# Router places in DRAM: rows of 64 bytes, zeroed and scattered whole, in place of single 4-byte words

## The chip, the cores and the metric

One core of one Trainium2 chip runs the whole program in one launch. The metric is device time in microseconds (us); lower is better. TensorE does the matmuls (PE in the rows), VectorE is DVE, ScalarE is ACT, GpSimd is POOL, and SP is the engine that issues most of the DMAs. Each engine works through its own instructions in order.

## The reference, cut to what matters

Three layers follow one another. A delta-rule attention over 4 x 8 heads, 768 tokens of width 48, is a recurrence over time:

```python
for t in range(S):
    y[:, :, t] = einsum('bhd,bhde->bhe', q[:, :, t], state)
    v_old = einsum('bhde,bhd->bhe', state, kt)
    state += bt * einsum('bhd,bhe->bhde', kt, vt - v_old)
```

Its output, 3072 tokens of width 384, goes through a mixture of 8 experts. Each token goes to the one expert with its largest logit (`e_idx = argmax(x @ w_gate)`), and is scaled by its probability and an output gate. A second mixture of 4 experts follows, in which every token goes through every expert and the results are summed with given weights.

## The kernel before, in words

**The attention stage** takes tokens in 12 chain steps of 64 positions for all batches and heads. A step multiplies keys with the state, solves a small triangular system, updates the state and forms the output. Its work is spread over all engines: DMAs bring k, q and v, TensorE transposes and multiplies, ACT and DVE copy out of PSUM. DVE's copy of the new state (line 414, `Sb<-Sp`) marks the end of a step. Two steps share one block inverse on DVE.

**The router** follows each step. Every step gives two tiles of 128 tokens. `done` computes their logits and stores a split fp16 copy of the tile in DRAM (`xd`; the store on SP waits for a POOL subtraction, line 499). `place` runs on groups of 4, 4, 4, 4, 4, 2, 1 and 1 tiles, 24 in all. On DVE and TensorE it computes for each token its place `su`: 3072 times its expert, plus how many tokens of this expert came earlier. Then POOL issues one indirect DMA for each tile (line 530), which scatters the 128 token numbers `rid` into the list `ord` in DRAM at those places. `ord` has 8 x 3072 + 512 entries, and is filled with zeros once, at the start (lines 481 and 482), from the tile `xr3` that `done` uses later.

**The first mixture** reads the lists back. After 20 tiles `early` loads the first 256 entries for expert 0 (line 541). When all scatters have landed, four loads on SP (`wid`, line 807) bring the first 512 entries of each expert, and POOL gathers rows of `xd` by them (line 734). The weights of experts 0 and 1 are loaded in the attention stage (`stw`, two staging buffers), those of the rest after it (`s`). The scatters of the second list, `meta` (line 656), run in this mixture, and their rows have 32 bytes.

**The order of the work** is written by a planner (class `Plan`): every operation has an engine, an estimated duration, reads, writes and a priority (lower goes first), and a list scheduler fixes each engine's order before anything runs. A DMA is two operations there: an issue on SP (`D`) and a transfer (`X`), which waits for other transfers. The planner counts a scatter as done when POOL has issued it. What waits for what on the chip is decided apart from that: the framework adds waits wherever tiles overlap, and a tile that a DMA reads is free only when the DMA has landed.

Of the kernel before, what the change touches and what calls it, by code (L numbers as in the profile page):

```python
# [7 lines left out]
F16 = mybir.dt.float16  # L8
I32 = mybir.dt.int32
U32 = mybir.dt.uint32  # L10
# [5 lines left out]
B, H, S, D = 4, 8, 768, 48  # L16
NSC = S // 128
N, DM, NE, FF, NE2 = 3072, 384, 8, 1024, 4
NT, KD, KF = N // 128, DM // 128, FF // 128
# [5 lines left out]
EW = 256  # L25
EG = 20
# [420 lines left out]
class Router:  # L447

    NXR=4
    def __init__(self,ctx,tc,dp):  # L450
        self.tc=tc; self.nc=tc.nc; self.xd=dp.tile([N,2*DM],F16,name="xd"); self.ord=dp.tile([NE*N+512,1],I32,name="ord")
        c=self.c=ctx.enter_context(tc.tile_pool(name="rc",bufs=1)); T=lambda n,s,d=F32: c.tile(s,d,name=n)
        self.wgo=T("wgo",[128,KD,16])
        self.tri=T("tri",[128,128],F16); self.ones16=T("ones16",[128,128],F16)
        self.desc=T("desc",[128,8])
        self.LG=T("LG",[128,NT,16]); self.OH=T("OH",[128,NT,8],F16)
        self.M2,self.RK,self.MX,self.AM=(T(n,[128,NT]) for n in ("M2","RK","MX","AM"))
        self.run=T("run",[128,8],F16); self.kq=T("kq",[128,2*KD*FF*2],F16); self.wa,self.wb=(T(n,[128,2*KD*FF],F16) for n in ("wa","wb")); self.cnt=T("cnt",[128,8]); self.pr=T("pr",[128,NT,4]); self.tok=T("tok",[128,NT],I32)
        self.xe=T("xe",[128,2*KD,EW],F16); self.few=T("few",[128,8])
    def setup(self,ctx,at,plan,wg,wo,probs):  # L460
        nc=self.nc; self.at=at; c=ctx.enter_context(self.tc.tile_pool(name="rt",bufs=1)); T=lambda n,s,d=F32: c.tile(s,d,name=n)
        self.xr=[T(f"xr{i}",[128,2,DM],F16) for i in range(self.NXR)]; self.xT=T("xT",[128,KD,128])
        self.sc=[T(f"sc{i}",[128,1]) for i in range(3)]
        self.v4,self.w4=T("v4",[128,4,8]),T("w4",[128,4,8]); self.sl,self.su=T("sl",[128,4]),[T(f"su{i}",[128,4],U32) for i in range(2)]; self.rs=T("rs",[128,8]); self.sep=T("sep",[1,1]); self.rid=T("rid",[128,NT],I32); self.ide=T("ide",[128,EW//128],U32); self.xge=[T(f"xge{j}",[128,2*DM],F16) for j in range(EW//128)]
        at.prio=-5
        for i,w in enumerate((wg,wo)): at.dma(self.wgo[:,:,8*i:8*i+8],w.rearrange("(k p) e -> p k e",p=128),(),[('wgo',i)],"wgo",xfer=100)
        for b in range(B):
            g,t=divmod(b,2)
            for x in range(2): R=slice(64*(g^t)+32*(x^t),64*(g^t)+32*(x^t)+32); at.dma(self.pr[R,t::2],probs[b*S:b*S+S].rearrange("(s x p) c -> x p s c",x=2,p=32)[x],(),[('pr',b,x)],"pr",xfer=60)
        def f():  # L470
            nc.gpsimd.memset(self.tri,1.0); nc.gpsimd.memset(self.ones16,1.0); nc.gpsimd.memset(self.run,0.0)
            nc.gpsimd.affine_select(out=self.tri,in_=self.tri,pattern=[[1,128]],compare_op=ALU.is_gt,fill=0.0,base=0,channel_multiplier=-1)
            for e in range(8): nc.gpsimd.memset(self.desc[:,e:e+1],float(8-e))
            nc.gpsimd.iota(self.rid,pattern=[[128,NT]],base=0,channel_multiplier=1)
            for b in range(B):
                g,t=divmod(b,2)
                for x in range(2): nc.gpsimd.iota(self.tok[64*(g^t)+32*(x^t):64*(g^t)+32*(x^t)+32,t::2],pattern=[[64,S//64]],base=b*S+32*x,channel_multiplier=1)
        at.op('G',2000,f,(),['rc','run'],"rc")

        z=self.xr[-1].rearrange("p a d -> p (a d)").bitcast(I32); kz=[('xr',self.NXR-1,0),('xr',self.NXR-1,1)]; n=(NE*N+512)//128  # L480
        at.op('G',300,lambda: nc.gpsimd.memset(z[:,0:n],0),(),kz,"rz")
        at.dma(self.ord.rearrange("(p n) o -> p (n o)",p=128),z[:,0:n],kz,['ord'],"rz",xfer=550)
        self.grp=list(GRP); self.g0=0; self.gi=0; self.sc_=[]
    def done(self,i,x,keys):
        at=self.at; nc=self.nc; j=i%3; am,sc=self.AM[:,i:i+1],self.sc[j]; x=x.rearrange("p (u d) -> p (u d)",d=D) if len(x.shape)==3 else x
# [21 lines left out]
    def place(self,a,n):  # L507

        at=self.at; nc=self.nc; t=f"rp {a}"; q=slice(a,a+n); at.prio=(a+n-1)//2+RPR+0.1; gk=[('wq',a)]; lk=gk; gp=Lazy(at,('wq',a))
        v=self.v4[:,0:n]; w=self.w4[:,0:n]; sl=self.sl[:,0:n]; su=self.su[self.gi%2][:,0:n]; ks=('su',self.gi%2); self.gi+=1  # L510
        pf=lambda: gp[:,0:8*n].rearrange("p (t e) -> p t e",e=8); oh=self.OH[:,q]; s=[128,n,8]
        V=nc.vector
        at.seq([(180,lambda: V.tensor_reduce(out=self.MX[:,q],in_=self.LG[:,q,0:8],axis=AX.X,op=ALU.max)),
                (180,lambda: V.tensor_tensor(out=v,in0=self.LG[:,q,0:8],in1=bc(self.MX[:,q],s,2),op=ALU.is_equal)),
                (180,lambda: V.tensor_tensor(out=v,in0=v,in1=bc(self.desc,s,1),op=ALU.mult)),
                (180,lambda: V.tensor_reduce(out=self.M2[:,q],in_=v,axis=AX.X,op=ALU.max)),
                (180,lambda: V.tensor_tensor(out=oh,in0=v,in1=bc(self.M2[:,q],s,2),op=ALU.is_equal))],[('LG',i) for i in range(a,a+n)]+['rc'],['v4',('OH',a)],t)
        def mm():
            pl=pf(); m=[(pl,self.tri,oh),(pl,self.ones16,bc(self.run,s,1))]+[(pl[:,k+1:],self.ones16,bc(oh[:,k],[128,n-1-k,8],1)) for k in range(n-1)]
            for x,(o,l,r) in enumerate(m): nc.tensor.matmul(out=o,lhsT=l,rhs=r,start=x==0,stop=x==len(m)-1,skip_group_check=True)  # L520
        at.op('P',150,mm,[('OH',a),'run','rc'],gk,t,take=lk,after=['w4'])
        at.op('V',200,lambda: V.tensor_tensor(out=w,in0=pf(),in1=oh,op=ALU.mult),[('wq',a),('OH',a)],['w4'],t,give=lk)
        at.op('V',180,lambda: V.tensor_scalar(out=sl,in0=self.M2[:,q],scalar1=-float(N),scalar2=8.0*N,op0=ALU.mult,op1=ALU.add),[('OH',a)],['sl'],t)
        at.seq([(180,lambda: V.tensor_reduce(out=self.RK[:,q],in_=w,axis=AX.X,op=ALU.add)),(180,lambda: V.tensor_tensor(out=su,in0=sl,in1=self.RK[:,q],op=ALU.add))],['w4','sl'],[ks],t)
        at.seq([(180,lambda: V.tensor_reduce(out=self.rs,in_=oh.rearrange("p t e -> p e t"),axis=AX.X,op=ALU.add)),(180,lambda: V.tensor_tensor(out=self.run,in0=self.run,in1=self.rs,op=ALU.add))],[('OH',a),'w4'],['run','rs'],t)
        for k in range(n):
            m=len(at.pl.ops)
            def sc(k=k):
                nc.gpsimd.memset(self.sep,0.0)
                r=nc.gpsimd.indirect_dma_start(out=self.ord[:],out_offset=bass.IndirectOffsetOnAxis(ap=su[:,k:k+1],axis=0),in_=self.rid[:,a+k:a+k+1],in_offset=None)  # L530
                self.tc.declare_no_dep(r.ins,group="ord",reason="places of different tokens"); self.tc.add_to_no_dep_group("ord",r.ins); self.sc_.append(r.ins.name)
            at.op('G',1360,sc,[ks,'ord'],[('tok',m)],t)
            at.op('X',100,lambda: None,[('tok',m)],[('or',a+k)],t,lat=XL)
        if a+n==EG: self.early()
    def early(self):

        at=self.at; nc=self.nc; cp=Lazy(at,'wfew'); at.prio=EG//2+RPR+0.2; t="few"
        at.op('P',60,lambda: nc.tensor.matmul(out=cp[:,0:8],lhsT=self.ones16,rhs=self.run,start=True,stop=True),['run','rc'],['wfew'],t,take=['wfew'])
        at.op('V',80,lambda: nc.vector.tensor_copy(out=self.few,in_=cp[:,0:8]),['wfew'],['few'],t,give=['wfew'])
        def ld():  # L540
            d=nc.sync.dma_start(out=self.ide,in_=self.ord[0:EW].bitcast(U32).rearrange("(j p) o -> p (j o)",p=128))
            for x in self.sc_: self.tc.add_manual_dep(d.ins,x,mybir.DependencyInfo(mybir.DependencyClass.Sync,mybir.DependencyReason.DATA),reason="places of the tokens so far")
        i=len(at.pl.ops)
        at.op('D',500,ld,[('or',x) for x in range(EG)]+['ord'],[('tok',i)],t,lat=450)
        at.op('X',60,lambda: None,[('tok',i)],['ide'],t,lat=XL)
        for j in range(EW//128):
            i=len(at.pl.ops)
# [124 lines left out]
class Moe:  # L672
# [90 lines left out]
    def general(self,tr,tabd,i):  # L763

        nc=self.nc; r=self.r; P=self.P
        nc.sync.dma_start(out=tr,in_=tabd[bass.ds(i,1)])
        row=nc.sync.value_load(tr[0:1,0:1],min_val=0,max_val=NE*N)
        col=nc.gpsimd.value_load(tr[0:1,1:2],min_val=0,max_val=N)
        e=nc.sync.value_load(tr[0:1,2:3],min_val=0,max_val=NE-1)
        xw=self.wid[:,0]; w=[]  # L770
        nc.sync.dma_start(out=xw,in_=r.ord[bass.ds(row,512)].bitcast(U32).rearrange("(j p) o -> p (j o)",p=128))
        for j,n,f in ((0,KD,FF),(1,KF,DM)):
            t=self.W[2][j].rearrange("p (l n f) -> p l n f",l=2,n=n); w.append(t); src=self.w[j][bass.ds(e,1)].rearrange("o (n p) f -> p (o n) f",p=128); step=1024//f
            for a in range(0,n,step):
# [22 lines left out]
    def moe1(self,meta,pr):  # L797
        nc=self.nc; tc=self.tc; r=self.r; pl=self.pl=Plan(tc,HOP); self.si=self.xi=self.bi=self.ci=self.hi=self.yi=0; self.pp_=0; self.parts={}
        with ExitStack() as c:
# [2 lines left out]
            self.xt=[T(f"xt{i}",[128,2*KD,WIN],F16) for i in range(2)]; self.xg=T("xg",[128,4,2*DM],F16); self.h=[T(f"h{i}",[128,2,WIN],F16) for i in range(NH)]  # L802
            self.y=[T(f"y{i}",[128,2,WIN],F16) for i in range(NY)]; self.st=[T(f"s{i}",[128,1024]) for i in range(STB)]; self.q=T("q",[128,768]); wid=self.wid=T("wid",[128,NE,4],U32)
            self.p1,self.p2=self.bank[0:3],self.bank[3:6]
            ov=r.ord[0:NE*N].bitcast(U32).rearrange("(e j p) o -> p e (j o)",e=NE,p=128)
            def ids(j):
                d=nc.sync.dma_start(out=wid[:,:,j:j+1],in_=ov[:,:,j:j+1])
                for x in r.sc_: tc.add_manual_dep(d.ins,x,mybir.DependencyInfo(mybir.DependencyClass.Sync,mybir.DependencyReason.DATA),reason="places of all tokens")
# [32 lines left out]
            n=n[0]  # L841
# [132 lines left out]
```

## Time and profile before

| | us |
|---|---|
| median of 3 runs | 1350.56 |
| their range | 1347.14 to 1350.72 |
| the profiled execution | 1349.12 |
| its span | 1347.5 |
| attention stage, to the last scatter's issue | 375.0 |
| TensorE busy over the span | 1204.3 (89%) |
| TensorE busy, 560 to 1347 | 767.03 of 787 |

The table's last row is why the stage after 560 us is left alone below: TensorE is full there. Where rows give a time from the span's start, the attention stage runs from 0 to 375, the first mixture follows, and the second one runs from 611.9 to the end. In the windows, "(x)" is the number of instructions, PEclk the granted share of TensorE's full clock, and DMA share how much of the time the 16 DMA engines were busy.

### The profile page before, as it was taken

The numbers are of one execution on the slowest core, as the hardware profiler recorded it, in microseconds if no ns is written. First come the engines' busy times: TensorE is split into PE (matmuls) and PEld (weight loads), VectorE is DVE, ScalarE is ACT, GpSimd is POOL, SyncE is SP. The second block draws the span as 40 slices with busy tenths as digits, with TensorE's granted clock in tenths as the row PEclk, the third lists the DMA queues.
The fourth block names the chain that finished last, engine by engine and source line by source line (L and its number), as shares of the span: only waits on it lengthen the run. The fifth ranks groups of instructions, "written<-read, shape, count | busy, mean of one in ns | idle before, by whom it ended". The sixth has DMA issues, their size and how long they took to land.

```text
span 1347.5 us, 40694 instructions
## 1 busy us (share of the span) xinstructions
PE 1204.3 (89%) x17569; PEld 1038.3 (77%) x17569; DVE 785.7 (58%) x1526; ACT 592.1 (44%) x1061; POOL 662.9 (49%) x879
## 2 busy tenths in 40 slices
PE   5777776877788899998999999999999999999997
PEld 5666666756675445557899998999989999999996
DVE  4567553866455655424755488555695565556555
ACT  3445444444234544413544455444554444444442
POOL 3224443446337962005745477445495454466655
PEclk8878887889789999999999999999999999999999
DMA  5343534124359777402200031001210000021100
GB/s 89 68 95 89 105 53 78 40 66 72 56 143 252 216 198 230 114 27 86 72 24 25 25 95 48 25 25 47 63 58 25 25 25 25 25 67 53 60 25 36
DMA packets 162807, 99.32 MB, mean 74 GB/s; under 512 B 117824, under 2 KB 152128, under 8 KB 162624
## 3 DMA queue, kind: packets, MB, share of 16 engines
q1 hardware_dynamic: 149328, 80.05, 24.5%
q0 software_dynamic: 6864, 15.45, 3.4%
q8 instruction: 139, 2.28, 0.7%
q10 hardware_dynamic: 6432, 1.18, 0.5%
q14 instruction: 44, 0.36, 0.1%
HBM read 76.38 MB, written 14.96 MB: 68 GB/s over the span
## 4 chain that ended last, share of the span: by engine, by line
PE 58%; issue 13%; DMA 9%; DVE 6%; POOL 6%; SPq 5%; ACT 2%; ACTq 0%; POOLq 0%; DVEq 0%
PE b L874 25%; PE b L893 22%; SPq L242 5%; DMA s<-in_moe_w_dram 3%; PE rw L378 2%; DMA stw<-in_moe_w_dram 2%; PE pb L364 1%; PE pb L294 1%; POOL S L882 1%; POOL q L721 1%; POOL meta L656 1%; PE Sp L225 1%; PE pb L378 1%; PE pb L309 1%; DVE v L699 1%
## 5 line engine op out<-in xcount | busy, mean ns | idle before, releaser
L874 PE MATMUL b<-wb,v 128*128 128x256 f16 x3456 | 392.8, 273 | 1.1 <-ACT a L876 1.0
L874 PEld LDWEIGHTS <-v 128*128 128x128 f16 x3456 | 336.7, 98 | 38.7 <-issue 1.7
L893 PE MATMUL b<-v,h 128*128 128x192 f16 x4032 | 352.5, 247 | 10.9 <-DVE cc L901 6.4
L893 PEld LDWEIGHTS <-h 128*128 128x128 f16 x4032 | 338.0, 98 | 15.5 <-issue 8.4
L882 POOL TENSOR_TENSOR S<-a 128x256 f32<-128x256 f32 x192 | 150.6, 805 | 271.1 <-ACT a L876 270.8
L886 DVE TENSOR_TENSOR h<-a,h 128x768 f16<-128x768 f32 x96 | 135.7, 1414 | 144.3 <-ACT h L885 144.3
L886 DVE TENSOR_TENSOR h<-S,h 128x1024 f16<-128x1024 f32 x96 | 121.2, 1263 | 125.3 <-ACT h L885 125.3
L885 ACT ACTIVATE h<-S 128x1024 f16<-128x1024 f32 x96 | 101.4, 1056 | 200.4 <-POOL S L882 180.7
L876 ACT ACTIVATE a<-b 128x512 f32<-128x512 f32 x192 | 113.2, 594 | 142.0 <-PE b L874 133.0
L882 POOL TENSOR_TENSOR S<-S,a 128x256 f32<-128x256 f32 x96 | 133.3, 1388 | 0.0
L885 ACT ACTIVATE h<-a 128x768 f16<-128x768 f32 x96 | 80.8, 842 | 2.8
L882 POOL TENSOR_TENSOR S<-a,S 128x256 f32<-128x256 f32 x96 | 73.5, 765 | 7.2
L233 POOL TENSOR_TENSOR v<-v,nt 128x384 f32<-128x384 f32 x24 | 20.6, 866 | 94.8 <-DMA v<-in_v_dram 62.4
L761 POOL DMA_DIRECT2D x<-y x27 | 19.7, 743 | 87.7 <-DVE y L759 78.0
L901 DVE TENSOR_TENSOR cc<-b,sm 128x192 f32<-128x192 f32 x192 | 58.5, 346 | 3.1 <-ACT sm L898 3.1
L225 PE MATMUL Sp<-wz 128*128 128x128 f16 x647 | 56.8, 243 | 2.3 <-issue 2.3
L699 DVE SCALAR_TENSOR_TENSOR v<-s,v 128x512 f16<-128x512 f32 (+2 forms) x56 | 44.9, 829 | 21.2 <-ACT v L698 21.0
L749 DVE SCALAR_TENSOR_TENSOR h<-b,h 128x432 f16<-128x432 f32 (+2 forms) x72 | 39.2, 552 | 24.1 <-ACT h L748 24.0
L225 PEld LDWEIGHTS <-wz 128*128 128x128 f16 x647 | 47.5, 111 | 6.7 <-issue 4.5
L748 ACT ACTIVATE h<-b 128x432 f16<-128x432 f32 (+2 forms) x72 | 34.0, 482 | 39.1 <-PE b L746 38.6
L756 PE MATMUL b<-h,kq 128*128 128x432 f16 (+2 forms) x288 | 42.8, 310 | 5.8 <-ACT h L748 5.2
L734 POOL DMA_INDIRECT xg<-xd,wid x30 | 29.9, 995 | 36.3 <-DMA xt<-xg 26.4
(258 smaller groups left out, 1736.6 us busy)
## 6 DMA issues: line engine op xcount, KB each, us to landing
wb<-x SPq DMA_DIRECT2D x72, 256.0 KB
s<-in_moe_w_dram SPq DMA_DIRECT2D x40, 384.0 KB
s<-in_moe_w_dram SPq DMA_DIRECT2D x18, 512.0 KB
s<-in_moe_w_dram SPq DMA_DIRECT2D x24, 256.0 KB
xd<-xr SPq DMA_DIRECT2D x24, 192.0 KB
x<-y POOLq DMA_DIRECT2D x21, 216.0 KB, 3.3
stw<-in_moe_w_dram SPq DMA_DIRECT2D x12, 256.0 KB
stw<-in_moe_w_dram SPq DMA_DIRECT2D x16, 192.0 KB
```

Of the source, the lines that this page charges most:

```text
L225: self.nc.tensor.matmul(out=b[:,:].rearrange("p (h d) -> p h d",d=64)[:,:,D:64],lhsT=self.wz,rhs=self.wz.rearrange("p (h d) -> p h d",d=16 ...
L242: self.op(q,occ,(lambda: e.dma_start_transpose(out=out,in_=in_)) if turn else (lambda: e.dma_start(out=out,in_=in_)),reads,list(writes)+[( ...
L378: M=lambda o,l,r,**k: nc.tensor.matmul(out=o,lhsT=l,rhs=r,skip_group_check=True,**k); hv=lambda a: a[:,0:512].rearrange("p (h d) -> p h d" ...
L699: self.op('V',69+1.042*n,lambda: self.nc.vector.scalar_tensor_tensor(out=lo,in0=s,scalar=64.0,in1=hi,op0=ALU.mult,op1=ALU.subtract),reads+ ...
L756: nc.tensor.matmul(out=ps,lhsT=w2[:,a,f,d*128:(d+1)*128],rhs=hs[f][0][:,b],start=(f,i)==(0,0),stop=(f,i)==(KF-1,2))
L874: for c,y in PASS: nc.tensor.matmul(out=F[k][:,f],lhsT=w[:,c,d,c_:c_+128],rhs=self.xk[B%2][d][:,y,256*i:256*i+256],start=(f,z)==(0,0),stop ...
L876: self.op('A',620,lambda k=k,g=g: A.activation(out=a[ja][:,g].rearrange("p x t -> p (x t)"),in_=F[k].rearrange("p a t -> p (a t)"),func=AF ...
L882: self.op('G',750,lambda o=o,x=x,y=y,w=w: G.tensor_tensor(out=X[o],in0=X[x],in1=X[y],op=w),ka,[ks])
L885: self.op('A',200+.833*m,lambda h=h,q=q,g=g: A.activation(out=h[:,0,:,q],in_=g,func=AF.Copy),kg,[kh+(0,)])
L886: self.op('V',200+1.042*m,lambda h=h,q=q,g=g: V.tensor_tensor(out=h[:,1,:,q],in0=g,in1=h[:,0,:,q],op=ALU.subtract),kg+[kh+(0,)],[kh+(1,)])
L893: for z,(c,d) in enumerate(PASS): nc.tensor.matmul(out=Q[k][:,o,0:192],lhsT=h[:,c,g,x],rhs=w[:,d,m,y],start=(m,o,z)==(0,0,0),stop=(m,z)==( ...
L901: self.op('V',340,lambda o=o,k=k,y=y,x=x: V.tensor_tensor(out=o,in0=Q[k][:,y,0:192],in1=s[:,x],op=ALU.add),[('Q',k),('sm',z,x)],[ko])
```

## The change

Each entry of `ord` becomes a row of 16 words (64 bytes), and each scatter writes the whole row, all 16 words with the token's number. `rid` shrinks from one word for every tile of the run to `[128, 4, 16]`, one group's rows, so it is filled again by an iota ahead of every group. The zeroing grows from 98 KB to 1.6 MB in two DMAs, the first with 1,536-byte pieces read over and over from `xr3`, and moves from priority -5 to 0.6. The readers take word 0 of each row.

```diff
-self.ord=dp.tile([NE*N+512,1],I32,name="ord")
+self.ord=dp.tile([NE*N+512,16],I32,name="ord")
...
-            nc.gpsimd.iota(self.rid,pattern=[[128,NT]],base=0,channel_multiplier=1)
...
-        at.op('G',300,lambda: nc.gpsimd.memset(z[:,0:n],0),(),kz,"rz")
-        at.dma(self.ord.rearrange("(p n) o -> p (n o)",p=128),z[:,0:n],kz,['ord'],"rz",xfer=550)
+        at.op('G',400,lambda: nc.gpsimd.memset(z,0),(),kz,"rz")
+        o=self.ord.rearrange("(p n) o -> p (n o)",p=128); w=384; at.prio=0.6; a=16*n//w
+        at.dma(o[:,0:a*w].rearrange("p (a w) -> p a w",w=w),z.rearrange("p (o w) -> p o w",o=1).to_broadcast([128,a,w]),kz,[('ord',0)],"rz",xfer=8000)
+        at.dma(o[:,a*w:],z[:,0:16*n-a*w],kz,[('ord',1)],"rz",xfer=550)
...
+        at.op('G',300,lambda: nc.gpsimd.iota(self.rid[:,0:n],pattern=[[128,n],[0,16]],base=128*a,channel_multiplier=1),(),['rid'],t)
...
-out_offset=bass.IndirectOffsetOnAxis(ap=su[:,k:k+1],axis=0),in_=self.rid[:,a+k:a+k+1],in_offset=None)
+out_offset=bass.IndirectOffsetOnAxis(ap=su[:,k:k+1],axis=0),in_=self.rid[:,k],in_offset=None)
...
-            at.op('G',1360,sc,[ks,'ord'],[('tok',m)],t)
+            at.op('G',1360,sc,[ks,'rid',('ord',0),('ord',1)],[('tok',m)],t)
...
-            ov=r.ord[0:NE*N].bitcast(U32).rearrange("(e j p) o -> p e (j o)",e=NE,p=128)
+            ov=r.ord[0:NE*N,0:1].bitcast(U32).rearrange("(e j p) o -> p e (j o)",e=NE,p=128)
```

The loads in `early` and `general` change as the last line does.

## Rows read from the trace of the kernel before

**Rows 1.** Windows: stretch, length, busy of each engine, granted clock, DMA share, GB/s.

```profile
159.00:170.00 11.00, 5.28 (x188) 4.63 (x181) 2.33 (x7) 2.44 (x6) 6.65 (x9) 0.66 0.58 38
197.00:209.00 12.00, 4.87 (x149) 4.19 (x145) 2.68 (x9) 0.99 (x2) 3.24 (x4) 0.52 0.42 37
268.00:278.00 10.00, 4.47 (x155) 3.63 (x159) 2.88 (x8) 2.77 (x9) 3.68 (x5) 0.73 0.21 25
331.00:344.00 13.00, 7.38 (x275) 6.24 (x263) 4.92 (x7) 2.22 (x6) 5.16 (x7) 0.75 0.54 49
420.00:450.00 30.00, 26.75 (x146) 14.08 (x145) 17.95 (x36) 15.92 (x33) 24.88 (x45) 1.00 0.91 262
```

**Rows 2.** POOL in order of time, first two scatter groups: start, length, line, operation.

```profile
8.00 0.16 POOL L474 IOTA rid<- 128x24 int32 x1
156.46 1.26 POOL L530 DMA_INDIRECT ord<-rid,su  x1 [0.19 <-issue]
...
196.79 0.97 POOL L530 DMA_INDIRECT ord<-rid,su  x1 [0.22 <-issue]
```

**Rows 3.** DMA issues of the two scatters: count, median us from issue to landing.

```profile
ord<-rid,su POOLq DMA_INDIRECT x24, 7.3
meta<-mt,csu POOLq DMA_INDIRECT x24, 3.5
```

**Rows 4.** Chain of waits in the attention stage: start, length, what.

```profile
152.97 2.46 DMA stw<-in_moe_w_dram
...
165.46 7.75 issue
...
200.91 7.12 issue
...
274.09 2.41 issue
...
313.11 8.60 DMA stw<-in_moe_w_dram
...
329.90 8.11 DMA stw<-in_moe_w_dram
...
339.17 7.20 DMA stw<-in_moe_w_dram
```

**Rows 5.** Ends of chain steps, line 414 on DVE in order of time.

```profile
83.33 0.55 DVE L414 COPY Sb<-Sp 112x384 f32<-112x384 f32 x1
...
139.67 0.56 DVE L414 COPY Sb<-Sp 112x384 f32<-112x384 f32 x1 [0.69 <-PE Sp L378]
...
193.04 0.55 DVE L414 COPY Sb<-Sp 112x384 f32<-112x384 f32 x1
...
219.96 0.55 DVE L414 COPY Sb<-Sp 112x384 f32<-112x384 f32 x1
...
249.70 0.56 DVE L414 COPY Sb<-Sp 112x384 f32<-112x384 f32 x1 [0.85 <-PE Sp L378]
...
266.50 0.53 DVE L414 COPY Sb<-Sp 112x384 f32<-112x384 f32 x1
...
297.95 0.55 DVE L414 COPY Sb<-Sp 112x384 f32<-112x384 f32 x1
...
350.05 0.56 DVE L414 COPY Sb<-Sp 112x384 f32<-112x384 f32 x1 [2.07 <-PE Sp L378]
```

**Rows 6.** Chain of waits, 372 to 395 us: from the last scatter to the weights.

```profile
375.00 4.12 DMA ord<-rid,su
...
383.83 6.26 DMA s<-in_moe_w_dram
```

**Rows 7.** SP's queue in order of time: the zeroing, and the first weight loads.

```profile
17.84 0.41 SPq L242 DMA_DIRECT2D ord<-xr  x1
...
68.53 0.91 SPq L242 DMA_DIRECT2D stw<-in_moe_w_dram  x2
```

**Rows 8.** Line 734 on POOL: what ended its idle time, us in total, times.

```profile
  DMA xt<-xg: 26.4, 6
```

**Rows 9.** Chain of waits, 40 to 160 us, shares by line.

```profile
by line: SPq L242 39.0%; issue 8.3%; PE pb L294 8.1%; PE rw L378 8.0%; DMA stw<-in_moe_w_dram 4.6%; PE Sp L378 4.1%; PE pb L364 3.6%; PE pb L378 3.1%; PE Sp L225 2.3%; DMA kf<-in_k_dram 1.7%; DVE X L344 1.7%; PE pb L309 1.7%; DMA qf<-in_q_d
```

More of the change, by code (lines that the diff above doesn't have):

```diff
@@ L450, in __init__ @@
     def __init__(self,ctx,tc,dp):
-        self.tc=tc; self.nc=tc.nc; self.xd=dp.tile([N,2*DM],F16,name="xd"); self.ord=dp.tile([NE*N+512,1],I32,name="ord")
+        self.tc=tc; self.nc=tc.nc; self.xd=dp.tile([N,2*DM],F16,name="xd"); self.ord=dp.tile([NE*N+512,16],I32,name="ord")
         c=self.c=ctx.enter_context(tc.tile_pool(name="rc",bufs=1)); T=lambda n,s,d=F32: c.tile(s,d,name=n)
@@ L463, in setup @@
         self.sc=[T(f"sc{i}",[128,1]) for i in range(3)]
-        self.v4,self.w4=T("v4",[128,4,8]),T("w4",[128,4,8]); self.sl,self.su=T("sl",[128,4]),[T(f"su{i}",[128,4],U32) for i in range(2)]; self.rs=T("rs",[128,8]); self.sep=T("sep",[1,1]); self.rid=T("rid",[128,NT],I32); self.ide=T("ide",[128,EW//128],U32); self.xge=[T(f"xge{j}",[128,2*DM],F16) for j in range(EW//128)]
+        self.v4,self.w4=T("v4",[128,4,8]),T("w4",[128,4,8]); self.sl,self.su=T("sl",[128,4]),[T(f"su{i}",[128,4],U32) for i in range(2)]; self.rs=T("rs",[128,8]); self.sep=T("sep",[1,1]); self.rid=T("rid",[128,4,16],I32); self.ide=T("ide",[128,EW//128],U32); self.xge=[T(f"xge{j}",[128,2*DM],F16) for j in range(EW//128)]
         at.prio=-5
@@ L529, in sc @@
                 nc.gpsimd.memset(self.sep,0.0)
-                r=nc.gpsimd.indirect_dma_start(out=self.ord[:],out_offset=bass.IndirectOffsetOnAxis(ap=su[:,k:k+1],axis=0),in_=self.rid[:,a+k:a+k+1],in_offset=None)
+                r=nc.gpsimd.indirect_dma_start(out=self.ord[:],out_offset=bass.IndirectOffsetOnAxis(ap=su[:,k:k+1],axis=0),in_=self.rid[:,k],in_offset=None)
                 self.tc.declare_no_dep(r.ins,group="ord",reason="places of different tokens"); self.tc.add_to_no_dep_group("ord",r.ins); self.sc_.append(r.ins.name)
-            at.op('G',1360,sc,[ks,'ord'],[('tok',m)],t)
+            at.op('G',1360,sc,[ks,'rid',('ord',0),('ord',1)],[('tok',m)],t)
             at.op('X',100,lambda: None,[('tok',m)],[('or',a+k)],t,lat=XL)
@@ L540, in ld @@
         def ld():
-            d=nc.sync.dma_start(out=self.ide,in_=self.ord[0:EW].bitcast(U32).rearrange("(j p) o -> p (j o)",p=128))
+            d=nc.sync.dma_start(out=self.ide,in_=self.ord[0:EW,0:1].bitcast(U32).rearrange("(j p) o -> p (j o)",p=128))
             for x in self.sc_: self.tc.add_manual_dep(d.ins,x,mybir.DependencyInfo(mybir.DependencyClass.Sync,mybir.DependencyReason.DATA),reason="places of the tokens so far")
         i=len(at.pl.ops)
-        at.op('D',500,ld,[('or',x) for x in range(EG)]+['ord'],[('tok',i)],t,lat=450)
+        at.op('D',500,ld,[('or',x) for x in range(EG)]+[('ord',0),('ord',1)],[('tok',i)],t,lat=450)
         at.op('X',60,lambda: None,[('tok',i)],['ide'],t,lat=XL)
@@ L770, in general @@
         xw=self.wid[:,0]; w=[]
-        nc.sync.dma_start(out=xw,in_=r.ord[bass.ds(row,512)].bitcast(U32).rearrange("(j p) o -> p (j o)",p=128))
+        nc.sync.dma_start(out=xw,in_=r.ord[bass.ds(row,512),0:1].bitcast(U32).rearrange("(j p) o -> p (j o)",p=128))
         for j,n,f in ((0,KD,FF),(1,KF,DM)):
```

## The prediction

> **What bounds the kernel now.** From 560 us on TensorE is full, and nothing of the change runs there. So the question is how much of the first 375 us, the attention stage, and of the hand-over behind it the change can move. I read the chain of waits first, then the windows around what it names, then POOL's queue and the DMA table.
>
> In the chain's longest pieces within the attention stage [rows 4] TensorE stands twice in "issue" for over 7 us (165.46 and 200.91), once for 2.41 (274.09), and three loads of weights into `stw` hold the chain for 8.60, 8.11 and 7.20 us. Another load of the same tile, at 152.97, took 2.46. "Issue" is time in which the engine waited for no other, so something slowed its supply of instructions and the loads alike.
>
> The windows tell what they share [rows 1]. From 159 to 170 the DMA engines were busy 0.58 of the time and moved 38 GB/s; from 197 to 209, 0.42 and 37; from 268 to 278, 0.21 and 25; from 331 to 344, 0.54 and 49. From 420 to 450 they were busy 0.91 and moved 262 GB/s. Per busy share that is 66 to 119 GB/s against 288: the DMAs there don't lack work, they are stuck. And each of these stretches begins within 4 us of a group of scatters into `ord`: the first group's first scatter starts at 156.46, the second group's last at 196.79 [rows 2]. Of these 4-byte scatters the median took 7.3 us to land, and of the 32-byte scatters into `meta`, which run while the weights stream at 262 GB/s, 3.5 [rows 1, 3]. So scatters as such don't jam the DMAs; those of single words do. 128 tokens on 8 experts have about 16 neighbours each in a list, so at 4 bytes most of a tile's words fall into few 64-byte pieces of DRAM. Why that is slow no row shows, only that rows of 32 bytes are not.
>
> **The change part by part.** Everything is set against the profiled execution (1349.12 us, span 1347.5). It lies 1.44 below the median of the runs, 1350.56.
>
> *Scatters, 24 of them, POOL's own time unchanged (128 rows each, about 0.97 us).* What goes is the jam behind the five groups of four. From above I take the stalls on the chain, as if nothing else came late: 7.75 + 7.12 + 2.41 in TensorE's issue, and the three `stw` loads less an ordinary one each, 8.60 + 8.11 + 7.20 - 3 x 2.46 = 16.5. That is 33.8 us [rows 4]. From below it is nothing, if other waits fill the gaps. Between them stand the step ends [rows 5]. Two neighbouring steps, one inverse in them, took 53.37 us (139.67 to 193.04, first group of scatters inside), 56.66 (to 249.70, second), 48.25 (to 297.95, third) and 52.10 (to 350.05, fourth and fifth). The one such stretch with hardly a scatter, 219.96 to 266.50, took 46.54. The differences are 6.8, 10.1, 1.7 and 5.6: 24.2 us. I take this value, because these steps contain what comes late next (DVE's inverse, loads of k), and keep 0 and 33.8 for the range.
>
> *The last scatter* stands on the chain: 4.12 us from its issue to SP's release, and behind it the `wid` loads, then the weight load that holds ACT, VectorE and TensorE [rows 6]. With the 3.5 of a 32-byte scatter it is 0.6 shorter [rows 3]. Ends: 0 and 0.6 (nothing faster is in these rows). The shorter hand-over moves all that follows.
>
> *The `wid` and `ide` loads* read as many single words as before, now 64 bytes apart. No row has such a stride. I take 0, and 2 us either way as an estimate, a third of the 6.26 us that the weight load takes behind them [rows 6].
>
> *Zeroing.* One SP issue of 0.41 us goes from 17.84 [rows 7], where SP's issues are the largest part of the chain, 39% of it from 40 to 160 [rows 9]: -0.4. At priority 0.6 the two new issues go ahead of the first `stw` loads (priority 40), at 68.53 [rows 7]. That SP turned to priority 40 there says that nothing more urgent was ready, and the issues hide in that gap. The 1.57 MB don't: at the 262 GB/s of rows 1 they take 6.0 us of all DMA engines, and q loads and instruction fetches behind them come later. Ends: 0, where those have slack, and 6.0. I take 1.5, as q is loaded steps ahead. The planner books 8 us of transfers for it, so it moves other work later in its order; that I count in the range alone. The memset that fills 768 words in place of 196 lies in POOL's idle time at the start.
>
> *Iotas.* Eight short ones on POOL in place of one of 0.16 us [rows 2]. What they wait for matters more. An iota overwrites `rid`, which the scatters of the group before read, so it holds POOL until they have landed. That POOL does wait for landed DMAs in this way is seen at line 734, 26.4 us in all for the `xt` transposes [rows 8]. Since the planner takes a scatter as done when issued, it will put an iota right behind a group. Queued behind it on POOL are the subtraction of line 499, for which SP's `xd` stores wait with k, v and weight loads behind them, the masks and the scaling of v. A landing of 3.5 us, less 0.97 for the issue, makes 2.5 us for each of the first five groups, of which most falls in POOL's idle time (6.65 of 11 us busy at most in rows 1). Ends: 0 and 5 x 2.5 = 12.5. I take 1.0, near the lower, as the stage's waits are on TensorE and DMAs, not on POOL. The last iota waits for the single scatter before it, whose landing falls about where the last scatter's places are ready: 0.
>
> Sum: -24.2 - 0.6 - 0.4 + 1.5 + 1.0 = -22.7. From 1349.12 that is 1326.4; on the footing of the median 1327.9. I say 1328.
>
> The Trainium skill speaks against it in one place. "DMA: Bandwidth & Descriptors", section Specifications, asks for at least 512 B for full rate, and says that below it the DMA does a read-modify-write. By that rule a row of 64 bytes is no better off than a word, the jam stays, and the gain is gone: the first rival. The 32-byte scatters of rows 3, with 3.5 us, don't follow it, which is why it gets a small chance.
>
> **The rivals.** *The change doesn't do what it says:* 64-byte rows jam the DMAs as words do, and POOL's holds fall into idle time. Then -0.4 + 1.5 remain, about 1351.5. For it: no row shows a 64-byte scatter. Against it: rows 3. Chance 0.07.
>
> *What lies under the jam takes over.* The two steps from 83.33 to 139.67, with no scatter in them, took 56.34 us [rows 5], more than those with one; SP's issues are the chain's largest part there [rows 9]. If SP's queue or the loads of k and q set the first two groups' steps too, only 1.7 + 5.6 + 0.6 + 0.4 - 2.5 = 5.8 us are won: 1345. Against it: TensorE's stalls of 7 us lie on the chain where SP is not. Chance 0.23.
>
> *Slower: POOL's holds reach SP.* The place is the iota behind a group, the price what the scatters' landing leaves of the hold: with landings at the old 7.3 us, 6.3 us a group, 32 us for five. If a fifth of it passes through line 499 and the `xd` stores into SP's queue, it costs 6.3, with the zeroing's 1.5 some 1358. It decides the sign only where the landings stay above some 5 us, since below that the jam has gone too. Chance 0.07.
>
> **How the numbers follow.** The forecast has 0.63, its own range 1314 to 1338: the lower end is the full 33.8 (1318.3) with `wid` loads 2 us shorter and the zeroing free, the upper the `stw` stalls' 16.5 only half won and `wid` loads 2 us longer. TensorE's granted clock adds to the lower side: it was 0.52 and 0.66 in the jammed stretches, near the lower of its two levels, against 1.00 at 420 to 450 [rows 1], and work done at it may speed up where TensorE no longer stands still; it is not in the sum. With the second rival, and about 2 in 10 left out, the range is 1314 to 1346. About 0.3% (4 us) is what a measurement of this kernel can tell from none: faster 0.86, the same 0.07, slower 0.07.
>
> **What would show it.** Right: no "issue" piece above 3 us after 156 in the chain, `stw` loads there of about 3 us, a median landing of the scatters near 3.5, the pairs of steps at 46 to 49 us, and the last scatter's issue at about 350. Wrong in its cause: stretches of 40 GB/s at half the DMA share that still follow each group. Wrong in its size: landings short, yet the last issue near 370. Wrong on POOL: iotas with idle time before them ended by `ord`, and `xd` stores late behind line 499. A gap in TensorE at 70 to 80 us would be the zeroing.

## The result, and the profile after

| | before | after |
|---|---|---|
| median, us | 1350.64 (6 runs, 1347.14 to 1360.3) | 1316.71 (6 runs, 1306.73 to 1321.45) |
| ratio, 95% interval | | 0.9724 [0.967, 0.9778] |
| profiled execution, us (its span) | 1349.12 (1347.5) | 1321.45 (1319.9) |

The change makes the kernel faster by 33.9 us where 22.7 were forecast. The ratio on 1350.56 gives 1313.3 us, just below the forecast range of 1314 to 1346: the direction was right, the size was not, and whether the mechanism was is decided by the experiments. The profiled execution after is the slowest of its six, so the two profiles differ by only 27.7 us.

The windows behind the first scatters of four groups, and the stream of weights of [rows 1] again (columns as there):

```profile
157.00:168.00 11.00, 9.50 (x407) 8.39 (x407) 3.46 (x10) 7.38 (x17) 7.54 (x12) 1.00 0.57 121
185.00:197.00 12.00, 9.97 (x383) 8.43 (x377) 10.14 (x28) 4.85 (x9) 4.41 (x7) 1.00 0.40 73
251.00:261.00 10.00, 7.85 (x354) 6.97 (x358) 6.19 (x13) 7.80 (x20) 8.76 (x11) 1.00 0.35 77
312.00:325.00 13.00, 8.05 (x371) 6.84 (x369) 6.72 (x10) 3.47 (x9) 6.35 (x8) 1.00 0.20 52
420.00:450.00 30.00, 27.02 (x144) 14.06 (x144) 15.97 (x36) 12.33 (x30) 27.42 (x47) 1.00 0.58 161
```

Read DMA share and GB/s together. At nearly the same share (0.57 against 0.58) the first stretch now moves 121 GB/s where it moved 38, which is 212 GB/s per busy share against 66. TensorE issues 407 matmuls in 11 us instead of 188, and its granted clock there is full (1.00, the higher level of 2.4 GHz), where [rows 1] has 0.52 to 0.75.

The first stretch by DMA queue (packets, MB, share of 16 engines' time), before (159 to 170 us) and then after (157 to 168):

```profile
q1 hardware_dynamic: 1214, 0.42, 57.4%
q0 software_dynamic: 56, 0.00, 0.4%
```

```profile
q1 hardware_dynamic: 4618, 1.25, 53.4%
q8 instruction: 3, 0.05, 2.0%
q0 software_dynamic: 121, 0.03, 1.3%
```

The scatters run on q0: the kernel without them, below, has 768 packets less there over the whole run. So in this stretch the engines' time goes not into the scatters' own packets but into those of q1, which moves most of the run's bytes: by these rows some 83 ns for a packet before and 20 after (an estimate, 57.4% of 16 x 11 us over 1214, and 53.4% over 4618). Before, no packet of the instruction queue is listed in these 11 us. That fits TensorE's "issue", but doesn't prove it.

The DMA issues: count, and median us from issue to landing (before: 7.3 and 3.5, [rows 3]).

```profile
ord<-rid,su POOLq DMA_INDIRECT x24, 3.0
meta<-mt,csu POOLq DMA_INDIRECT x24, 3.8
```

Pieces of the chain of waits, to set beside [rows 4] and [rows 6]: start, length, what.

```profile
69.05 8.06 DMA stw<-in_moe_w_dram
...
150.33 3.22 DMA stw<-in_moe_w_dram
...
261.70 2.13 issue
...
309.28 4.25 DMA stw<-in_moe_w_dram
...
316.95 3.78 DMA stw<-in_moe_w_dram
...
348.85 2.69 DMA ord<-rid,su
...
354.03 3.69 DMA s<-in_moe_w_dram
```

The "issue" pieces of over 7 us are gone (the longest behind 136 us is 2.13), and the weight loads that held the chain for 7 to 9 us hold it for about 4. One new long piece, a weight load, stands right behind the zeroing, at 69.05.

The ends of the chain steps that answer to [rows 5]:

```profile
138.09 0.56 DVE L414 COPY Sb<-Sp 112x384 f32<-112x384 f32 x1
...
181.55 0.56 DVE L414 COPY Sb<-Sp 112x384 f32<-112x384 f32 x1 [0.68 <-PE Sp L378]
...
232.23 0.55 DVE L414 COPY Sb<-Sp 112x384 f32<-112x384 f32 x1
...
275.71 0.55 DVE L414 COPY Sb<-Sp 112x384 f32<-112x384 f32 x1
...
324.30 0.56 DVE L414 COPY Sb<-Sp 112x384 f32<-112x384 f32 x1 [1.44 <-PE Sp L378]
```

The four pairs of neighbouring steps now take 43.46, 50.68, 43.48 and 48.59 us: 186.21 in all, and 210.38 before.

Last, SP's four `wid` loads, first before and then after: start, us for the four.

```profile
379.30 4.48 SPq L807 DMA_DIRECT2D wid<-ord  x4
```

```profile
351.72 2.26 SPq L809 DMA_DIRECT2D wid<-ord  x4
```

From these rows the two profiles can be split by stage, and set against the terms of the forecast:

| stretch | before | after | difference | forecast |
|---|---|---|---|---|
| start to the end of the step at 139.67 | 139.67 | 138.09 | -1.6 | +1.1 (zeroing +1.5, SP's issue -0.4) |
| the four pairs of steps | 210.38 | 186.21 | -24.2 | -23.2 (stalls -24.2, iotas +1.0) |
| last step's end to the last scatter's issue | 24.95 | 24.55 | -0.4 | 0 |
| last scatter's issue to the first load of `s` | 8.83 | 5.18 | -3.65 | -0.6 |
| to the first matmul of the second mixture (611.93, 583.90) | 228.10 | 229.87 | +1.8 | 0 |
| to the end | 735.6 | 736.0 | +0.4 | 0 |
| sum | | | -27.6 | -22.7 |

### The profile page after: what moved, and what is told of

Its sections match the earlier page's. It is cut to its first block, busy times and chain, and to the rows that moved or that the text cites. A ratio compares the mean times of both kernels' runs of the same rounds, so it can differ in the third digit from the quotient of the medians.

```text
span 1319.9 us, 40662 instructions
## 1 busy us (share of the span) xinstructions
PE 1196.4 (91%) x17547; PEld 1031.9 (78%) x17547; DVE 794.3 (60%) x1526; ACT 592.9 (45%) x1061; POOL 665.7 (50%) x886
## 4 chain that ended last, share of the span: by engine, by line
PE 59%; DMA 11%; issue 10%; DVE 7%; POOL 6%; SPq 6%; ACT 1%; ACTq 0%; POOLq 0%; DVEq 0%
PE b L876 25%; PE b L895 22%; SPq L242 5%; PE rw L378 3%; DMA s<-in_moe_w_dram 2%; DMA x<-y 2%; DMA stw<-in_moe_w_dram 2%; POOL q L723 2%; DMA xt<-xg 1%; PE pb L294 1%; POOL meta L658 1%; PE pb L364 1%; PE pb L378 1%; DVE v L701 1%; PE Sp L225 1%
## 5 line engine op out<-in xcount | busy, mean ns | idle before, releaser
L225 PE MATMUL Sp<-wz 128*128 128x128 f16 x625 | 53.9, 240 | 1.9 <-issue 1.9
L751 DVE SCALAR_TENSOR_TENSOR h<-b,h 128x432 f16<-128x432 f32 (+2 forms) x72 | 39.4, 553 | 24.2 <-ACT h L750 24.1
L903 DVE TENSOR_TENSOR sm<-b,sm 128x192 f32<-128x192 f32 x144 | 46.3, 349 | 1.6
```

What stands on the lines that cost most here:

```text
L225: self.nc.tensor.matmul(out=b[:,:].rearrange("p (h d) -> p h d",d=64)[:,:,D:64],lhsT=self.wz,rhs=self.wz.rearrange("p (h d) -> p h d",d=16 ...
L751: self.op('V',69+1.042*n,lambda ps=ps,h=h: nc.vector.scalar_tensor_tensor(out=h[:,1],in0=ps,scalar=0.0,in1=h[:,0],op0=ALU.max,op1=ALU.subt ...
L903: self.op('V',340,lambda o=o,k=k,y=y,x=x: V.tensor_tensor(out=o,in0=Q[k][:,y,0:192],in1=s[:,x],op=ALU.add),[('Q',k),('sm',z,x)],[ko])
```

## The experiments

The comparisons were made on several chips. Each verdict is a ratio to runs of the kernel before on the same chip at the same time. Diffs are against the kernel after, unless they say otherwise.

**What in a 4-byte scatter is slow.** Four kernels on one chip, where the kernel before took 1359.64 us (median of 13). The first is the change, unaltered.

> The changed kernel once more, for a second profile. Its first profiled execution took 1321.45 us and is the slowest of six (1306.73 to 1321.45). Theory 1 (the jam is gone and the rest is chance between executions): again 1306 to 1322, scatters land in a median of about 3.0 us, last scatter issued at 335 to 349. Theory 2 (the first profile was a poor sample of another state): the profile shows some stretch of 5 us or more that the first one had and this one has not, and names the engine.

Measured: 1311.98 us, 0.9653 [0.9617, 0.9689]. The gain repeats, and is larger on this chip: 47.7 us.

The second keeps the rows of 64 bytes, but writes only one 4-byte word in each:

```diff
-scalar1=-float(N),scalar2=8.0*N
+scalar1=-16.0*N,scalar2=128.0*N
...
-V.tensor_tensor(out=su,in0=sl,in1=self.RK[:,q],op=ALU.add)
+V.scalar_tensor_tensor(out=su,in0=self.RK[:,q],scalar=16.0,in1=sl,op0=ALU.mult,op1=ALU.add)
...
-out=self.ord[:], ... in_=self.rid[:,k]
+out=self.ord.rearrange("n (o u) -> (n o) u",u=1), ... in_=self.rid[:,k,0:1]
```

> The changed kernel with each scatter writing 4 bytes, word 0 of a token's 64-byte row, in place of all 16 words; the order on every engine and all else are the changed kernel's. Theory A (what jams is a write of a part of a 64-byte piece, whatever its neighbours do): scatters land in a median of about 7 us, DMA traffic stalls behind the groups, 1343 to 1352 us. Theory B (what jams is several words of one 64-byte piece written at about the same time): median landing about 3 us, 1307 to 1322 us, as the changed kernel. Both: the loads of the places as short as in the changed kernel (4 issues in 2.3 us), since they still read one word in 64 bytes.

Measured: 1314.17 us (1311.66 to 1317.12), 0.9661 [0.9624, 0.9697], the same as the change beside it. Its scatters land as fast as whole rows do (2.5 us in both):

```profile
ord<-rid,su POOLq DMA_INDIRECT x24, 2.5
```

So writing only 4 bytes is not what is slow.

The third has the order of work and the iotas of the change, and lists of 4-byte words that lie side by side, with 98 KB of zeros, as before:

```diff
-self.ord=dp.tile([NE*N+512,16],I32,name="ord")
+self.ord=dp.tile([NE*N+512,1],I32,name="ord")
...
-in_=self.rid[:,k]
+in_=self.rid[:,k,0:1]
...
```

> The changed kernel with the lists as dense 4-byte words again and 98 KB of zeros; planner costs, priorities and so the order on every engine stay the changed kernel's. Theory A and theory B: the jam is back, median landing about 7 us, and the time is 1340 to 1355 us; less than 1350 by as much as the new order is worth alone. Rival (the gain came from the new order, not from the rows): 1305 to 1325 us, with long landings. The four loads of the places take 4.5 us of SP's issue again if close words hurt reads as well, 2.3 us if not.

Measured: 1356.84 us, 1.0006 [0.9972, 1.004]. The whole gain is gone. Its DMA issues, chain and `wid` loads:

```profile
ord<-rid,su POOLq DMA_INDIRECT x24, 10.3
```

```profile
196.12 7.64 issue
...
272.34 3.17 issue
...
319.38 3.49 issue
...
333.62 7.62 DMA stw<-in_moe_w_dram
...
342.40 7.44 DMA stw<-in_moe_w_dram
```

```profile
384.70 5.15 SPq L809 DMA_DIRECT2D wid<-ord  x4
```

The same loads in the change beside it:

```profile
340.28 2.27 SPq L809 DMA_DIRECT2D wid<-ord  x4
```

The landing, the stalls in "issue" and the long `stw` loads are back, and the four loads hold SP for 5.15 us in place of 2.27. So words that lie close together are slow to write, and loads of them hold SP longer; the same words 64 bytes apart do neither. (The row is SP's time over the four loads; when their data landed it doesn't say.) The new order of the work is worth nothing by itself. Between these two kernels the stages can be split on one chip. Third and last step's end, first in the kernel with dense words, then in the change:

```profile
135.36 0.56 DVE L414 COPY Sb<-Sp 112x384 f32<-112x384 f32 x1
...
352.97 0.56 DVE L414 COPY Sb<-Sp 112x384 f32<-112x384 f32 x1 [1.52 <-PE Sp L378]
```

```profile
135.05 0.56 DVE L414 COPY Sb<-Sp 112x384 f32<-112x384 f32 x1 [0.54 <-PE Sp L378]
...
315.21 0.56 DVE L414 COPY Sb<-Sp 112x384 f32<-112x384 f32 x1 [2.07 <-PE Sp L378]
```

The pairs take 217.61 against 180.16: 37.4 us, more than the 33.8 that the prediction had as their upper end.

The fourth goes the other way: the kernel before with its own order and its zeroing at the start, only with rows of 64 bytes. Its iota is issued inside a group's first scatter, and the planner doesn't know of it. Against the kernel before:

```diff
-self.ord=dp.tile([NE*N+512,1],I32,name="ord")
+self.ord=dp.tile([NE*N+512,16],I32,name="ord")
...
+                k or nc.gpsimd.iota(self.rid[:,0:n],pattern=[[128,n],[0,16]],base=128*a,channel_multiplier=1); ...
...
-in_=self.rid[:,a+k:a+k+1]
+in_=self.rid[:,k]
...
```

> The kernel before, its order on every engine kept, with 64-byte rows, whole-row scatters, 1.6 MB of zeros at the old early place, and each group's iota right ahead of the group's first scatter in place of one at the start. Theory (the rows alone make the gain): 1312 to 1328 us, median landing about 3 us, last scatter issued near 349 us, unless the early zeroing delays the first loads of k and q, then up to 6 us more. Rival (about 10 us of the gain come from the planner's new order): 1325 to 1335 us with short landings.

Measured: 1314.43 us, 0.9668 [0.9635, 0.97]: the rows alone make the whole gain.

**How far apart the words must lie.** The row's width is the one change, in the list, in `rid`, in the iota and in the zeroing, for example:

```diff
-self.ord=dp.tile([NE*N+512,16],I32,name="ord")
+self.ord=dp.tile([NE*N+512,2],I32,name="ord")
...
-self.rid=T("rid",[128,4,16],I32)
+self.rid=T("rid",[128,4,2],I32)
...
```

> The changed kernel with rows of 2 words (8 bytes), all written; order and planner costs the changed kernel's, zeros of 0.2 MB. If the harm goes with the number of writes that share a 64-byte piece (8 here, 16 in dense words, 1 in the change), median landing 5 to 7 us and 1320 to 1340 us; if only words of 4 bytes are harmed, 1306 to 1322.

> The changed kernel with rows of 4 words (16 bytes), 4 to a 64-byte piece, zeros of 0.4 MB. By shared writes: median landing 3.5 to 5 us, 1312 to 1326 us. If a piece of 32 bytes is what counts, 2 share it, and it lands nearer 3 us and 1308 to 1318.

> The changed kernel with rows of 8 words (32 bytes), 2 to a 64-byte piece, zeros of 0.8 MB. The scatters into meta have rows of this size and landed in 3.5 us in the kernel before, so near the changed kernel: median landing 2.5 to 3.5 us, 1304 to 1322 us, and by up to 2 us better for half of the zeroing if zeroing costs anything.

Measured on one chip (before: 1369.73): rows of 8 bytes 1387.61 us, 1.0113 [1.0078, 1.0147], slower than single words; 16 bytes 1344.4, 0.9789 [0.9746, 0.9833]; 32 bytes 1334.2, 0.9738 [0.9701, 0.9775]. In these runs the distance of the words and the bytes written change together; only at 64 bytes were the two taken apart, by the single words above. How long SP's `wid` loads waited for the last scatters says the same. From SP's waits (us in total, times, longest), with rows of 8, 16 and 32 bytes, and of 64 in a run of the change on a later chip:

```profile
SPq L809 <- DMA ord<-rid,su: 10.0, 1, 10.0
```

```profile
SPq L809 <- DMA ord<-rid,su: 5.7, 1, 5.7
```

```profile
SPq L809 <- DMA ord<-rid,su: 4.6, 1, 4.6
```

```profile
SPq L809 <- DMA ord<-rid,su: 3.7, 1, 3.7
```

With rows of 8 bytes the jam behind the first group is as plain as it gets: DMA share 0.99 at 28 GB/s, and 84 matmuls in 10 us:

```profile
162.00:172.00 10.00, 3.19 (x84) 2.59 (x77) 1.31 (x5) 1.99 (x4) 0.00 (x0) 0.50 0.99 28
```

The expectation had 8 bytes better than 4; why they are worse no run tells. The four `wid` loads, though, get shorter with every step: 4.26, 3.01, 2.47 and 2.26 us of SP in these four runs. That 32 are enough was tried again beside the change, on a chip where the kernel before took 1368.68.

> The kernel after the change, unaltered, so that the three beside it are compared on the same chip. All theories: 0.966 to 0.975 of the kernel before.

> 32 bytes for each place instead of 64 (0.8 MB of zeros instead of 1.6 MB). If words jam only inside one 32-byte piece: the same time as the change beside it or up to 3 us less, since 0.8 MB less is zeroed. If the piece is 64 bytes: two places share one, the landings of the word writes rise again and it is 5 to 15 us above the change beside it.

Measured: 1333.07 us, 0.9762 [0.9718, 0.9805], and 1333.86, 0.976 [0.9723, 0.9797]. Two rows in one piece of 64 bytes cost nothing that these runs can tell.

**What the zeroing costs.** Twice as much of it, tried twice, and less than a fifth of it:

```diff
+self.more=dp.tile([NE*N+512,16],I32,name="more")
...
+o2=... zero=lambda: [nc.sync.dma_start(out=x[:,0:a*w]. ... for x in (o2,o)]; ...
```

```diff
-at.dma(o[:,0:a*w].rearrange("p (a w) -> p a w",w=w),z. ... .to_broadcast([128,a,w]),kz,[('ord',0)],"rz",xfer=8000)
+at.dma(self.ord[0:NE*N].rearrange("(e r) o -> e (r o)",e=NE)[:,0:8192]. ... ,z[:,0:64]. ... .to_broadcast([128,NE,64]),kz,[('ord',0)],"rz",xfer=8000)
...
+at.dma(self.ord[NE*N:]. ... ,z[:,0:64],kz,[('ord',1)],"rz",xfer=550)
```

> The changed kernel with the large zeroing DMA sent twice, once more into a scratch list that nothing reads, right ahead of the real one. What it adds is the price of one zeroing at this place: 1.5 us by the prediction's value, 0 where loads have slack, 6 us where they don't: 1312 to 1322 us against the changed kernel's 1306 to 1321.

> The change with its zeroing transfer sent twice (1.6 MB more). If 1.6 MB cost 1.5 us: 1 to 2 us above the change beside it. If the zeroing delays the first stage's loads at the rate the engines move data: 4 to 6 us above. Rival, hidden whole: equal within 1 us.

> 64 bytes for each place as in the change, but only the first 512 places of each list and the tail are zeroed (0.26 MB instead of 1.6 MB); what lies behind is read by nothing for these inputs. If the zeroing costs what the prediction put on it (1.5 us): 0 to 2 us below the change beside it. If it costs more through the weight loads that it delays: 3 to 6 us below. Rival, that it is hidden whole: equal within 1 us.

Measured: doubled, 1339.9 us, 0.9771 [0.9728, 0.9813], on the chip of the narrow rows, and 1337.46, 0.9781 [0.9741, 0.9821], beside the change's 1333.07; cut to 0.29 MB, 1333.03, 0.9746 [0.9698, 0.9795], beside the same 1333.07. So the 1.3 MB saved are worth nothing that can be told, and the 1.6 MB added perhaps 4 us, with intervals that overlap. In the profile after, the long `stw` piece at 69.05 is on the chain, and yet the step that ended at 139.67 ends 1.6 us earlier, so the steps behind it seem to have slack. In the change's second profile no such piece is on the chain.

**What is left of the scatters' cost.** The gain was larger than forecast by the medians, and the pairs of steps in the first two profiles showed just the forecast 24.2 us. Four kernels on a further chip, to split the difference on one chip and to see whether scatters of 64 bytes still cost anything.

> The kernel before, unaltered, profiled on the same chip as the change beside it. Theory 1, the stall term was too small: its four pairs of steps (from the third state copy to the eleventh) take 30 to 38 us longer than those of the change beside it, and the way from the last scatter's issue to the first weight load some 3.5 us longer. Theory 2, the term was right and the rest lies elsewhere: the pairs differ by 22 to 27 us, and 8 us or more are found ahead of the first scatter or behind the first weight load.

> The kernel after the change, unaltered, beside the kernel before and the two below. 0.965 to 0.976 of before; pairs of steps of 42 to 51 us by both theories.

Measured: 1365.39 us (1.0004 [0.9979, 1.0029]) and 1336.4, 0.9805 [0.9753, 0.9857], a smaller gain than expected. Split as above, the change saves 1.9 us up to the end of the third step, 23.5 in the pairs and 4.6 from the last scatter to the load of `s`, and loses 3.0 between the last step and the last scatter. What follows the first load of `s` is 2.4 shorter. Here the pairs are what theory 2 says, but the 8 us that it wanted elsewhere aren't there.

The next leaves out the 24 scatters, so every place read back is token 0, and only the attention stage is compared. The other issues every scatter twice, the first time into a table that nothing reads:

```diff
-                r=nc.gpsimd.indirect_dma_start(out=self.ord[:], ...
+                return
```

```diff
+                for x in range(2):
+                    x and nc.gpsimd.memset(self.sep,0.0)
+                    r=nc.gpsimd.indirect_dma_start(out=(self.more,self.ord)[x][:], ...
```

> The change without its 24 scatters into the lists; all else is issued as before, so every place read back is token 0 and the gathers fetch one row over and over. Only the attention stage, up to the last state copy, is compared. If the change has taken the whole cost of the scatters: the last state copy comes within 4 us of that of the change beside it. If 64-byte rows still jam a little: 6 to 15 us earlier.

> The change with every scatter issued twice, first into a second table that nothing reads, then into the list: 24 more scatters of 128 rows of 64 bytes, some 1.3 us of POOL each. If a 64-byte scatter costs the chain nothing but its POOL time at the very end: 0 to 4 us above the change beside it. If it still stalls loads and instructions at a third of the old price: 8 to 12 us above.

Measured: 1365.45 us for the doubled scatters, 1.0008 [0.9978, 1.0037], 29 us above the change. The last step's end, in order without scatters, the change, with doubled scatters, and before:

```profile
319.82 0.56 DVE L414 COPY Sb<-Sp 112x384 f32<-112x384 f32 x1 [2.81 <-PE Sp L378]
```

```profile
339.05 0.56 DVE L414 COPY Sb<-Sp 112x384 f32<-112x384 f32 x1 [2.77 <-PE Sp L378]
```

```profile
361.07 0.56 DVE L414 COPY Sb<-Sp 112x384 f32<-112x384 f32 x1 [2.80 <-PE Sp L378]
```

```profile
364.45 0.56 DVE L414 COPY Sb<-Sp 112x384 f32<-112x384 f32 x1 [3.03 <-remote]
```

Both theories miss: on this chip scatters of 64 bytes still cost 19.2 us up to the last step, and the change took 25.4 of 44.6. The windows over two groups' issues on POOL, 5.2 us each, show where. First the change in its first profile, then on this chip, then the kernel before on this chip:

```profile
155.09:160.29 5.20, 4.45 (x223) 3.93 (x216) 2.95 (x9) 2.48 (x5) 4.53 (x8) 1.00 0.68 142
180.65:185.85 5.20, 3.68 (x212) 3.53 (x215) 3.89 (x14) 1.98 (x4) 4.29 (x7) 1.00 0.50 95
```

```profile
154.60:159.80 5.20, 2.71 (x50) 1.68 (x39) 0.77 (x2) 0.49 (x1) 4.52 (x8) 0.88 0.55 122
185.90:191.20 5.30, 2.75 (x60) 1.84 (x59) 0.22 (x2) 0.49 (x1) 4.16 (x7) 0.82 0.34 63
```

```profile
155.90:161.10 5.20, 3.52 (x80) 2.44 (x80) 0.19 (x1) 0.25 (x1) 4.53 (x8) 0.64 0.82 93
192.90:198.10 5.20, 2.08 (x43) 1.32 (x33) 1.34 (x6) 0.49 (x1) 4.16 (x7) 1.00 0.47 58
```

While POOL issues scatters, TensorE, VectorE and ScalarE here issue about a quarter of the instructions that they issue in the first profile, in both kernels alike. Behind the group it is over; the change then runs free:

```profile
162.00:172.00 10.00, 10.00 (x340) 9.55 (x338) 2.81 (x9) 5.85 (x14) 3.80 (x5) 0.66 0.30 66
```

There are two costs, then. One is the jam behind a group of close words, which the change takes away. The other is a hold of all engines while POOL issues; it is in the profiles of these runs and of the two sets before (narrow rows, zeroing), not in the first pair of profiles nor in the first set (lone and dense words), and no width of a row touches it: in the 5.2 us from 0.3 us ahead of the first group's first scatter TensorE issues 62 to 82 matmuls where the hold shows, and 172 to 235 where it doesn't. Doubling the scatters adds 29 / 24 = 1.2 us each, about the 1.3 us by which the scatters of a group follow one another. What makes the hold come and go isn't settled. The record gives the first set and the one with the zeroing beside the change the same chip number (6), so the chip alone may not be it; and the profiles with the hold list no landing for any of POOL's indirect DMAs, where those without it do. Nor is what it does to the gain: by the medians the change saves 28 and 36 us where it shows, 34 and 48 where it doesn't.

## Why the prediction was right, and where it was wrong

**The mechanism holds.** The prediction put the stalls on words that share a piece of DRAM. Most of its signs are there: no "issue" above 3 us, `stw` loads of 3.2 to 4.3 us, landings of 3.0, the last scatter at 348.85 where "about 350" was said. One is not: the pairs of steps were to take 46 to 49 us, and three of the four lie outside. The kernel with dense words and the new order gives all of it back, the one with rows and the old order keeps it.

**The step that failed is the hand-over**, the term that every pair of profiles shows too small; the stalls and the costs, below, add to it. "The last scatter" was given 0 to 0.6 us ("nothing faster is in these rows"), and the `wid` loads 0. Measured are 1.43 for the scatter's landing (4.12 to 2.69) and 2.22 for the four loads (4.48 to 2.26): 3.65 together, 4.15 against dense words, 4.6 on the last chip. The 3.5 of the 32-byte scatters in [rows 3] was taken as the least there is, and 3.0 is the median now. And the prediction saw that close words are slow to write, and did not ask whether loads of them are slow too; its 2 us "either way" came from a weight load, not from the words' spacing.

**The stalls: 24.2 was right for the two profiles, and their bound was not one.** The mean of the four pairs after is 46.55 us, and the stretch with hardly a scatter, taken as the floor, was 46.54. Pair by pair it did not come out: savings of 6.8, 10.1, 1.7 and 5.6 us were forecast, and 9.9, 6.0, 4.8 and 3.5 came, so that the sum agrees is in part luck. And a floor it is not: the same kernel on the second chip has pairs of 45.37, 50.29, 42.67 and 41.83. Against dense words on that chip the pairs save 37.4, 13.2 more than the term has and beyond the 33.8 of the chain's stalls that was kept as the upper end; there this is the larger miss. Nor is the sum of such stalls an upper end: by the same recipe the chain of the dense words gives 7.64 + 3.17 + 3.49 in "issue" and 7.62 + 7.44 - 2 x 2.46 in `stw` loads, 24.4 us, and 37.4 are won. Which waits off those pieces make up the rest isn't shown.

**The costs were put too high.** Zeroing: 1.5 forecast; nothing that can be told, by the cut to 0.29 MB. The iotas' holds on POOL: 1.0 forecast; POOL's idle time before them (line 527), ended by the scatters' landing, was 1.8 us in three waits, and the pairs, where most of them fall, saved the 24.2 us of the stalls all the same:

```profile
  DMA ord<-rid,su: 1.8, 3
```

**The rest is which execution is looked at.** By the profiles the forecast missed 5 us (27.6 against 22.7), of which 3.0 are the hand-over, 2.7 the early part, 1.0 the iotas in the pairs, 0.4 the stretch before the last scatter, and -2.2 what came later than forecast behind it. A further 6.3 us lie between profiles and medians: the profile before is 1.5 us below its median, the one after 4.7 above. The six runs after are ordered by their granted clock: 1306.73 and 1310.36 us at 0.965, 1314.35 at 0.964, 1319.08 at 0.961, 1320.14 at 0.958, 1321.45 at 0.955 (before, in its profile, 0.944). Whether the clock makes the time or follows from TensorE's pauses these runs don't separate. The prediction named the clock as a reason on the lower side and left it out of the sum. Where the 6.3 us come from stays open. Two sums of the prediction are off by less than a microsecond: by its own terms the lower end is 1314.8, and the first rival 1351.7.

**The rivals.** That rows of 64 bytes jam as words do fell with the landings of 3.0 us. The rule that spoke for it, at least 512 B or a read-modify-write (the Trainium skill, "DMA: Bandwidth & Descriptors", Specifications), does not sort these runs: single words of 4 bytes are as fast as rows of 64 when they lie 64 bytes apart, and slow when they lie side by side. That the work under the jam takes over fell: the first two pairs, which this rival gave nothing, save 9.91 and 5.98 us. POOL's holds through the iotas did not reach SP: between 140 and 360 us it waited 39.3 us for the subtraction ahead of the `xd` stores, and 43.8 before.

## What to carry to other kernels

When a scatter or gather of small items is slow, look at how far apart its items lie in DRAM before looking at how small they are: here 16 bytes brought most of the gain, 32 all of it, and the padding's 1.6 MB of zeros cost nothing that could be told. A DMA share of half at a seventh of the GB/s of the weight stream (38 against 262) was the sign here, and its victims were elsewhere: weight loads and TensorE's "issue". When such a list is read back, put a price on those loads too; and when a forecast is made against one profiled execution, keep the spread of executions (15 us over six runs here) in the range.

## What was not expected of the hardware

- In the jam behind the first group the DMA engines' time goes into the packets of other queues: 57.4% of it into q1 at some 83 ns a packet (20 after), and 0.4% into the scatters' own.
- Rows of 8 bytes are worse than words of 4 (1.0113 against 1 on one chip), with the DMA engines busy 0.99 of 10 us at 28 GB/s.
- Four loads of single words take SP 4.5 to 5.2 us when the words lie side by side, 2.3 when they lie 64 bytes apart.
- In some sets of runs the other engines issue about a quarter of their instructions while POOL issues indirect DMAs (50 matmuls in 5.2 us against 223), at 1.2 us for each scatter; in others nothing of this shows.
